# One attention-decode kernel: TensorE's two visits taken out of the loop around all engines, its closing branch followed by an aligned block, and five memsets moved from VectorE to GpSimd

## The chip, the cores and the metric

The kernel runs on one core of one Trainium2 chip. The metric is the device time of one execution in microseconds. The time before is the median of three runs. The profile is of one further execution of the same program: its span runs from the first to the last instruction that the profiler recorded in the kernel, and the execution's own time is longer than the span, because something lies ahead of the first instruction and behind the last one. The engines are named as in the profile: PE (TensorE; PEld is its weight loads), DVE (VectorE), ACT (ScalarE), POOL (GpSimd) and SP (SyncE, which issues nearly all DMAs here). A letter q behind a name (SPq, PEldq) marks work of the engine's sequencer: branches, register moves, semaphore waits, DMA issues.

## What is computed

One decode step for one token with 32 heads, a cache of 8192 positions and head size 128, all in float32, and beside it a gated unit:

```
xn = layernorm(x)                                   # x: 1 x 1 x 512
q  = (xn @ wq), 32 heads of 128
o  = softmax(q . k_cache * 128**-0.5) . v_cache     # 8192 positions per head
s  = o @ wo
g  = silu((sigmoid(xn @ w_gate) * (xn @ w_up)) @ w_down)
out = x + s * g
```

The two caches are 32 x 8192 x 128 float32 each, 134 MB apiece. With the weights the kernel reads 293.67 MB and writes 2 KB.

## The kernel before

**Tiling.** The heads are taken in 16 pairs. A pair's keys are one load of 8 MB into one of three slots of SBUF, 128 partitions by 16384 numbers; a pair's values are another such load. Keys alternate between slots 0 and 1, values go to slot 2; the last pair's keys and values come in halves.

**Stages of a pair.** DVE multiplies the keys in place by the pair's query (L380) and sums each row of 128 (L381), so that every partition holds 128 scores, and takes their maximum (L383). PE turns and spreads the maxima, ACT forms the powers with exp (L397), PE multiplies them with the values (32 matmuls onto `po`), ACT copies `po` (L402), PE picks the parts, and DVE scales and turns the pair's output (L387 to L390). `scores(i)` of one pair runs ahead of `heads_out(i - 1)` of the pair before.

**Start.** Before the first pair DVE clears some tiles (L217 to L232), cuts `pick` out of the identity (L234), turns `x` once its load has come (L241), and forms the layer norm; then it scales `wq` (L266, L267), and PE sums the columns into the queries. The gate's weights are treated the same way.

**End.** After the last pair PE multiplies the heads' outputs with `wo`, which comes in six loads (`W_ENDS`), DVE does the last product and sum (L471, L473), and SP stores the result (L489).

**Order of the loads.** SP issues everything in one order written by hand: `wq`, `w_gate`, `w_up`, the first keys; then each load behind a wait for the engine that frees its slot (`load_keys(i, summed[i - 2])`, `load_values(i - 1, (valued, i - 1))`).

**Control flow.** All engines run a block `body` that ends in a closing branch (L493) back to its own start; the register `once` is 0 at the start and 1 at the end, so the branch falls through and the body runs once. On ACT, DVE and PE a hint instruction further up names that branch ahead of time (`mark_branch_hint_location`). PE's instructions are written down with `Later`, an object that notes calls and plays them later. PE plays them inside the body so: a loop of two visits (L477) around a conditional block (L478). On visit 0 the block is skipped, so PE jumps to the loop's end and back; on visit 1 it runs `before` (everything up to the first pair) and then a loop of 15 rounds over `each` (one pair). Behind that loop stand PE's hint, `last` (the last pair) and `after` (the product with `wo`).

**Behind the closing branch** stands the block `done`: SP clears the semaphores (L501), all engines meet in a barrier (drains at L101), SP waits there for the result's store as well, and a second barrier of all engines (L528) ends the kernel.

The two visits in the code:

```
with nc.Fori(0, 2, engines=pe_only) as visit:
    with PE.engine.If(visit > 0):
        PE.play(before)
        with nc.Fori(0, NP - 1, engines=pe_only):
            PE.play(each)
hints[PE.engine] = PE.engine.mark_branch_hint_location()
PE.play(last)
PE.play(after)
```

Of the kernel before, what the change touches and what calls it, by code (L numbers as in the profile page):

```python
# [10 lines left out]
ALU = mybir.AluOpType  # L11
# [39 lines left out]
def kernel(  # L51
# [12 lines left out]
    nc = tc.nc  # L64
# [24 lines left out]

    W_ENDS, W_FOLD = (14, 24, 28, 30, 31, 32), 28  # L90

    DVE, ACT, SP, POOL = nc.vector, nc.scalar, nc.sync, nc.gpsimd
    PE = Later(nc.tensor)
    pe_only = OrderedEngineSet([nc.tensor.engine])

    s_out = tc.alloc_semaphore("s_out")
    ACT.nop().then_inc(s_out, 16)
    section = ctx.enter_context(ExitStack())  # L100
    section.enter_context(tc.tile_critical())  # L101

    def sb(name, *shape):
        return nc.alloc_sbuf_tensor(name, [P, *shape], F32)[:]
# [9 lines left out]
    pick, half = sb("pick", 2 * HT), sb("half", 2)  # L114
# [9 lines left out]
    weights = sb("weights", NB // HT, 2 * HT)  # L124
    sc = [sb(f"sc{i}", NB) for i in range(2)]
    on = sb("on", Dh)
# [28 lines left out]
    pe, dve, act, pool = (Steps(n) for n in ("s_pe", "s_dve", "s_act", "s_pool"))  # L155
# [10 lines left out]
    def wait(eng, *steps):  # L166
        for s in steps:
            if s is not None:
                eng.wait_ge(*s)
# [26 lines left out]
    def load_keys(i, *after):  # L196
        n = (i + 1) % 2
        wait(SP, *after)
        ld_k[i] = [(j, load(SP, f"k{n}_{j.start}", slots[n][:, cols(j)], rows_of(k_cache, i)[:, cols(j)]))
                   for j in (FULL if i < NP - 1 else HALVES)]  # L200

    def load_values(i, *after):
# [2 lines left out]
        SP.dma_start(slots[2], rows_of(v_cache, i)).then_inc(s_val, 16)  # L205

    load_keys(0)


    once = nc.alloc_registers("once")  # L210
    nc.regs_mov(once, 0)
    nc.br("body")
    body = ctx.enter_context(ExitStack())
    body.enter_context(nc.body("body"))
    hints = {e: e.mark_branch_hint_location() for e in (ACT, DVE)}

    c_xrow = dve(DVE.memset(x_row, 0.0))  # L217
    ld_xr = load(ACT, "xr", x_row[0:P:GP, :], xv.rearrange("(g c) -> g c", g=NG), c_xrow)
# [2 lines left out]
    c_id = pool(POOL.memset(ident, 0.0))  # L221
    wait(POOL, c_id)
    c_id = pool(POOL.affine_select(out=ident, in_=ident, compare_op=ALU.not_equal, fill=1.0, base=0,
                                   pattern=[[-1, P]], channel_multiplier=1))
    dve(DVE.memset(acc, 0.0))
    dve(DVE.memset(po, 0.0))
    dve(DVE.memset(weights, 0.0))
    dve(DVE.memset(on, 0.0))
    c_half = dve(DVE.memset(half, 0.0))
    wait(DVE, c_id, c_half)  # L230
    for e, h in enumerate(HALF):
        dve(DVE.memset(half[h, e:e + 1], 1.0))  # L232
    for g in range(NG):
        c_pick = dve(DVE.tensor_copy(pick[g * GP:(g + 1) * GP, :],  # L234
                                     ident[g * GP:(g + 1) * GP, g * GP:g * GP + 2 * HT]))
# [6 lines left out]
    t = dve(DVE.reduce_sum(st[:, 0:1], x_col, axis=AX.X))  # L242
    wait(PE, t)
    t = pe(PE.matmul(pt[:, 0:1], ones, st[:, 0:1], start=True, stop=True))
    wait(DVE, t)
# [6 lines left out]
    t = dve(DVE.reduce_sum(st[:, 2:3], sq, axis=AX.X))  # L252
    wait(PE, t)
    t = pe(PE.matmul(pm[:, 0:1], ones, st[:, 2:3], start=True, stop=True))
    wait(ACT, t, c_eps)
# [7 lines left out]
    def in_place(w, k, cols=slice(None)):  # L263
        y = w[:, 0, cols]
        if k == 0:
            return dve(DVE.tensor_scalar(y, y, xn[:, 0:1], None, op0=ALU.mult))  # L266
        return dve(DVE.scalar_tensor_tensor(y, w[:, k, cols], xn[:, k:k + 1], y, op0=ALU.mult, op1=ALU.add))  # L267
# [8 lines left out]
    for t in range(NQ):  # L276
        c = slice(t * QT, (t + 1) * QT)
        wait(PE, in_place(wq_t, KT - 1, c), copies.get(t - 2))
        spreads[t] = pe(PE.matmul(big[t % 2], ones, wq_t[:, 0, c], start=True, stop=True))
        wait(ACT, spreads[t])  # L280
# [74 lines left out]
                            start=(b == 0), stop=(b == HT - 1))  # L355
        ins.then_inc(picked, 1)

    wait(PE, c_pick, c_id)
    before = PE.take()
    pair(slots[2], {0: lambda: taken(s_val, 16)})  # L360
    each = PE.take()
# [112 lines left out]
    after = PE.take()  # L474


    with nc.Fori(0, 2, engines=pe_only) as visit:  # L477
        with PE.engine.If(visit > 0):  # L478
            PE.play(before)
            with nc.Fori(0, NP - 1, engines=pe_only):  # L480
                PE.play(each)
    hints[PE.engine] = PE.engine.mark_branch_hint_location()
    PE.play(last)
    PE.play(after)

    SP.wait_ge(s_out, 16)
    SP.nop().then_inc(s_out, -16)
    wait(SP, t)
    SP.dma_start(out.rearrange("a b (g c) -> (a b g) c", g=NG), g_row[0:P:GP, :]).then_inc(s_out, 16)  # L489

    nc.regs_alu(once, once, 1, op=ALU.add)
    for e in (ACT, DVE, PE.engine, POOL, SP):
        br = e.br_lt(once, 1, on_true="body", on_false="done")  # L493
        if e in hints:
            br.branch_hint(hints[e])
    body.close()
    nc.switch_bb("done")

    used = sorted(s.num for s in sems)
    assert used == list(range(used[0], used[0] + len(used)))  # L500
# [32 lines left out]
```

## Time and profile before

| | us |
|---|---|
| median of 3 runs | 689.98 (689.77 to 690.3) |
| the profiled execution, its own time | 690.04 |
| its span | 685.7 |
| own time less span | 4.3 |
| DVE busy | 606.2 (88% of the span) |
| PE busy | 211.8 (31%) |
| POOL busy | 0.7 (six instructions) |
| memory read | 293.67 MB, 428 GB/s over the span |

How to read it: an engine's busy time is that of its computing instructions alone. A wait is the idle time of an engine ahead of an instruction, with what ended it. The chain that ended last is followed back from the last instruction. For DMA queues the profile gives packets, megabytes and the time that the packets took as a share of 16 DMA engines over the stretch asked for. Queue q1 carries SP's loads, q10 the load of `x`, and q8 and q14 carry packets of the kind "instruction", that is, program text.

### The profile page before, as it was taken

How to read it: one execution, taken by the hardware profiler on the slowest of the kernel's cores; microseconds unless marked ns; L12 is line 12 of the kernel's file. 1: busy time of each engine (PE TensorE's matmuls, PEld its weight loads, DVE VectorE, ACT ScalarE, POOL GpSimd, SP SyncE). 2: the span in 40 equal slices, each digit the busy share in tenths (PEclk: the TensorE clock that was granted, in tenths of full speed). 3: DMA queues.
4: the chain of work that ended last, by engine and by line, in shares of the span. 5: the costliest groups of instructions: out<-in, count | busy, mean ns of one | idle time of the engine just before them, and what ended most of it. 6: DMA issues, size and time to landing. Idle time of an engine off the chain costs nothing.

```text
span 685.7 us, 3402 instructions
## 1 busy us (share of the span) xinstructions
PE 211.8 (31%) x1422; PEld 74.8 (11%) x1422; DVE 606.2 (88%) x166; ACT 39.9 (6%) x120; POOL 0.7 (0%) x6
## 2 busy tenths in 40 slices
PE   0242015060512306050512406050522406060476
PEld 0010001020101102020100101020100102010121
DVE  3876999999999899998989899898989899899931
ACT  0030010000010100000000100000010100000010
POOL 0000000000000000000000000000000000000000
PEclk9975557575665757575665757575575757575698
DMA  8999999999999999999999999999999999999996
GB/s 368 433 446 428 463 432 428 428 428 428 428 432 428 443 459 440 428 428 428 428 428 432 428 440 455 447 428 428 428 428 428 432 428 428 466 417 459 400 428 278
DMA packets 6610, 293.71 MB, mean 428 GB/s; under 512 B 744, under 2 KB 752, under 8 KB 1232
## 3 DMA queue, kind: packets, MB, share of 16 engines
q1 hardware_dynamic: 6600, 293.67, 99.1%
q8 instruction: 2, 0.03, 0.0%
q10 hardware_dynamic: 8, 0.00, 0.0%
HBM read 293.67 MB, written 0.00 MB: 428 GB/s over the span
## 4 chain that ended last, share of the span: by engine, by line
DVE 51%; DMA 35%; SPq 0%; issue 0%; PE 0%
DMA slot<-in_A_k_cache_dram 31%; DVE sc L381 25%; DVE slot L380 25%; DMA slot<-in_A_wo_dram 4%; SPq L163 0%; DVE on L388 0%; DVE o_t L390 0%; DVE mx L372 0%; DVE mx L383 0%; PE pt L37 0%; PE acc L37 0%; DVE g_row L471 0%; DVE g_row L473 0%; DVE rl L387 0%; DVE g_row L417 0%
## 5 line engine op out<-in xcount | busy, mean ns | idle before, releaser
L380 DVE TENSOR_TENSOR slot<-slot,q_all 128x16384 f32<-128x16384 f32 (+1 forms) x17 | 275.6, 16214 | 34.0 <-DMA slot<-in_A_k_cache_dram 34.0
L381 DVE TENSOR_REDUCE sc<-slot 128x128 f32<-128x16384 f32 (+1 forms) x17 | 275.7, 16216 | 0.6
L37 PE MATMUL po<-slot,weights 128*8 128x512 f32 x1024 | 146.8, 729 | 263.9 <-PEq L37 263.9
L37 PEld LDWEIGHTS po<-slot,weights 128*8 128x8 f32 x1024 | 45.5, 102 | 351.9 <-issue 345.1
L37 PE MATMUL pt<-ident,mx 128*1 128x128 f32 x32 | 8.6, 367 | 107.8 <-PEq L37 107.8
L402 ACT COPY o<-po 128x512 f32<-128x512 f32 x16 | 9.4, 587 | 416.9 <-PE po L37 416.9
L267 DVE SCALAR_TENSOR_TENSOR slot<-slot,xn 128x512 f32<-128x512 f32 (+2 forms) x16 | 24.3, 1554 | 3.0 <-DMA slot<-in_A_wq_dram 2.7
L37 PE MATMUL pn<-o,pick 128*2 128x128 f32 x128 | 16.5, 272 | 12.8 <-PEq L37 12.8
L37 PE MATMUL big<-slot,ones 128*128 128x512 f32 (+3 forms) x52 | 12.2, 496 | 25.5 <-DVE slot L267 23.6
L37 PEld LDWEIGHTS pt<-ident,mx 128*1 128x1 f32 x32 | 1.8, 80 | 112.0 <-issue 112.0
L37 PEld LDWEIGHTS pn<-o,pick 128*2 128x2 f32 x128 | 9.9, 84 | 29.5 <-issue 27.1
L387 DVE RECIPROCAL rl<-pn 2x1 f32<-2x1 f32 x16 | 2.3, 146 | 12.2 <-PE pn L37 12.2
L397 ACT ACTIVATE weights<-sc,nb 64x128 f32<-64x128 f32 x32 | 12.8, 401 | 0.9
L395 ACT ACTIVATE nb<-pm 128x2 f32<-128x2 f32 x16 | 2.8, 173 | 150.8 <-PE pm L37 150.8
L37 PE MATMUL pm<-mx,ones 1*128 1x2 f32 x32 | 8.6, 337 | 7.8 <-PEq L37 7.8
L471 DVE TENSOR_TENSOR g_row<-g_row,acc 128x128 f32<-128x128 f32 x1 | 0.3, 289 | 11.7 <-PE acc L37 11.7
L37 PE MATMUL pn<-rs,half 128*2 128x1 f32 x32 | 3.0, 163 | 23.7 <-PEq L37 23.7
L37 PE MATMUL big<-slot,o_all 128*1 128x512 f32 x56 | 8.9, 725 | 2.8 <-DMA slot<-in_A_wo_dram 2.8
L37 PE MATMUL big<-slot,o 128*1 128x512 f32 (+1 forms) x22 | 4.5, 934 | 16.3 <-DMA slot<-in_B_w_down_dram 16.3
L37 PEld LDWEIGHTS pm<-mx,ones 1*128 1x128 f32 x32 | 7.7, 298 | 14.6 <-issue 14.6
L37 PEld LDWEIGHTS big<-slot,ones 128*1 128x1 f32 (+1 forms) x52 | 4.0, 133 | 34.2 <-DVE slot L267 28.3
L283 ACT COPY q_all<-big 64x256 f32<-64x256 f32 x16 | 5.9, 368 | 23.1 <-PE big L37 22.6
(56 smaller groups left out, 52.5 us busy)
## 6 DMA issues: line engine op xcount, KB each, us to landing
slot<-in_A_wq_dram SPq DMA_DIRECT2D x2, 4096.0 KB, 18.2
slot<-in_A_k_cache_dram SPq DMA_DIRECT2D x2, 4096.0 KB, 37.8
slot<-in_A_v_cache_dram SPq DMA_DIRECT2D x2, 4096.0 KB, 37.8
slot<-in_A_wo_dram SPq DMA_DIRECT2D x1, 3584.0 KB, 15.4
slot<-in_B_w_gate_dram SPq DMA_DIRECT2D x1, 2752.0 KB, 28.9
slot<-in_B_w_up_dram SPq DMA_DIRECT2D x1, 2752.0 KB, 34.9
slot<-in_B_w_down_dram SPq DMA_DIRECT2D x1, 2560.0 KB, 22.0
slot<-in_A_wo_dram SPq DMA_DIRECT2D x1, 2560.0 KB, 21.1
```

The costliest lines, as they stand in the source:

```text
L37: ins = getattr(self.engine, name)(*args, **kwargs)
L267: return dve(DVE.scalar_tensor_tensor(y, w[:, k, cols], xn[:, k:k + 1], y, op0=ALU.mult, op1=ALU.add))
L283: copies[t] = act(ACT.copy(qb[h, 2 * t:2 * t + 2, :], q[h, :, e, :]))
L380: wait(DVE, dve(DVE.tensor_mul(k[:, j, :], k[:, j, :], qb[:, i:i + 1, :].to_broadcast([P, n, Dh]))))
L381: summed[i] = dve(DVE.reduce_sum(sc[i % 2][:, j], k[:, j, :], axis=AX.X))
L387: wait(DVE, dve(DVE.reciprocal(rl[:2], pn[:, Dh:])))
L395: wait(ACT, act(ACT.mul(nb, pm, -SCALE)))
L397: ACT.activation(weights[h, :, e * HT:(e + 1) * HT], sc[i % 2][h].rearrange("p (g b) -> p g b", b=HT), AF.Exp, bias=nb[h, e:e + 1], scale= ...
L402: ACT.copy(o1, po).then_inc(copied, 1)
L471: t = dve(DVE.tensor_mul(g_row, g_row, acc))
```

## The change

Four things are done.

1. All five engines' instructions in the body are noted with `Later` and played afterwards; only the first loads of SP (`first_loads`) are played ahead, where they stood. Each engine keeps its order.
2. PE's two visits come ahead of the body. A PE-only block `visit` skips its content while PE's register `pe_once` is 0, counts it up and jumps back while it is under 2. Only then do all engines go into `body`, which for PE now holds the hint, `last` and `after` alone. The other engines set `once` to 1 with a move ahead of the body, where they had set it to 0, and the addition at the end (L491) is gone on all engines.
3. Behind `done`, PE's next instruction is put at the start of a new block of 256 instructions (`addr_align(256)`); the gap is filled with no-ops.
4. The memsets of `weights`, `on` and `half` (one and two halves) go from DVE to POOL, behind POOL's work on the identity; PE's wait ahead of the first pair is for the last of them instead of the identity. DVE no longer waits for its own memset of `half`.

```diff
-    DVE, ACT, SP, POOL = nc.vector, nc.scalar, nc.sync, nc.gpsimd
-    PE = Later(nc.tensor)
+    DVE, ACT, SP, POOL, PE = (Later(e) for e in (nc.vector, nc.scalar, nc.sync, nc.gpsimd, nc.tensor))
...
-    ACT.nop().then_inc(s_out, 16)
+    nc.scalar.nop().then_inc(s_out, 16)
+    once = nc.alloc_registers("once")
+    pe_once = next(r for r in once if r.engine == nc.tensor.engine)
+    nc.reg_mov(pe_once, 0)
...
     load_keys(0)
-    once = nc.alloc_registers("once")
-    nc.regs_mov(once, 0)
-    nc.br("body")
-    body = ctx.enter_context(ExitStack())
-    body.enter_context(nc.body("body"))
-    hints = {e: e.mark_branch_hint_location() for e in (ACT, DVE)}
+    first_loads = SP.take()
...
-    dve(DVE.memset(weights, 0.0))
-    dve(DVE.memset(on, 0.0))
-    c_half = dve(DVE.memset(half, 0.0))
-    wait(DVE, c_id, c_half)
+    pool(POOL.memset(weights, 0.0))
+    pool(POOL.memset(on, 0.0))
+    wait(POOL, pool(POOL.memset(half, 0.0)))
     for e, h in enumerate(HALF):
-        dve(DVE.memset(half[h, e:e + 1], 1.0))
+        c_pool = pool(POOL.memset(half[h, e:e + 1], 1.0))
+    wait(DVE, c_id)
...
-    wait(PE, c_pick, c_id)
+    wait(PE, c_pick, c_pool)
...
-    with nc.Fori(0, 2, engines=pe_only) as visit:
-        with PE.engine.If(visit > 0):
+    SP.play(first_loads)
+    for r in once:
+        if r.engine != nc.tensor.engine:
+            nc.reg_mov(r, 1)
+    nc.br("visit", engines=pe_only)
+    with nc.body("visit", valid_engines=pe_only):
+        with PE.engine.If_ne(pe_once, 0):
             PE.play(before)
             with nc.Fori(0, NP - 1, engines=pe_only):
                 PE.play(each)
-    hints[PE.engine] = PE.engine.mark_branch_hint_location()
+        PE.engine.reg_alu(pe_once, pe_once, 1, ALU.add)
+        PE.engine.br_lt(pe_once, 2, on_true="visit", on_false="visited")
+    nc.switch_bb("visited")
+    nc.br("body")
+    body = ctx.enter_context(ExitStack())
+    body.enter_context(nc.body("body"))
+    hints = {e: e.mark_branch_hint_location() for e in (nc.scalar, nc.vector, nc.tensor)}
+    for e in (ACT, DVE, POOL, SP):
+        e.play(e.take())
     PE.play(last)
     PE.play(after)
+    SP = nc.sync
...
-    nc.regs_alu(once, once, 1, op=ALU.add)
...
     nc.switch_bb("done")
+    nc.tensor.addr_align(256)
```

More of the change, by code (lines that the diff above doesn't have):

```diff
@@ L489 @@
     SP.dma_start(out.rearrange("a b (g c) -> (a b g) c", g=NG), g_row[0:P:GP, :]).then_inc(s_out, 16)
-    nc.regs_alu(once, once, 1, op=ALU.add)
-    for e in (ACT, DVE, PE.engine, POOL, SP):
+    for e in (nc.scalar, nc.vector, nc.tensor, nc.gpsimd, nc.sync):
         br = e.br_lt(once, 1, on_true="body", on_false="done")
```

## The prediction

> **What bounds the kernel now.** I read the span first, then the windows by stage, then both ends, since the change touches only the two ends.
>
> ```profile
> span 685.7 us, 3402 instructions
> ```
>
> ```profile
> core 0: us, PE busy (x) PEld busy (x) DVE busy (x) ACT busy (x) POOL busy (x), PEclk, DMA share, GB/s
> 0.00:8.00 8.00, 0.00 (x0) 0.00 (x0) 2.15 (x14) 1.28 (x1) 0.70 (x6) 1.00 0.85 326
> 8.00:92.00 84.00, 18.26 (x80) 5.83 (x80) 66.53 (x34) 8.76 (x21) 0.00 (x0) 0.73 1.00 431
> 92.00:234.00 142.00, 44.84 (x311) 16.63 (x310) 141.34 (x25) 8.28 (x25) 0.00 (x0) 0.64 1.01 436
> 234.00:620.00 386.00, 116.57 (x781) 42.77 (x782) 357.57 (x74) 17.47 (x60) 0.00 (x0) 0.63 1.00 433
> 620.00:656.00 36.00, 11.61 (x80) 4.46 (x79) 35.83 (x10) 1.75 (x6) 0.00 (x0) 0.62 1.01 437
> 656.00:686.00 30.00, 20.56 (x174) 5.10 (x172) 2.81 (x12) 2.33 (x7) 0.00 (x0) 0.87 0.78 334
> ```
>
> The last two columns decide. From 8 to 656 us the DMA engines are full (share 1.00 or 1.01) at 431 to 437 GB/s. DVE is busy for nearly all of 92 to 234 us too, but the queue loses nothing by that. So the loads set the 648 us between, and no edit changes a load, its order or what it waits for. What is left to win or lose is how early the first load is issued, and what follows the last one.
>
> The end, from the chain of waits in order of time and from the lines of the closing branch (L493), the two barriers (L101, L528) and the store:
>
> ```profile
> 657.68 24.18 DMA slot<-in_A_wo_dram
> ...
> 681.91 0.44 PE acc L37 x8
> ...
> 682.70 0.29 DVE g_row L473
> ```
>
> ```profile
> 683.02 0.65 SPq L489 DMA_DIRECT2D out_dram<-g_row  x1
> ```
>
> ```profile
> L493 PEldq COMPARE_BRANCH  x1: 83/83/83, 682.0 to 682.0; - x1
> ```
>
> ```profile
> L101 SPq EVENT_SEMAPHORE  x4: 17/22/360, 684.0 to 684.3; - x4
> ...
> L101 PEldq DRAIN  x1: 8/8/8, 684.0 to 684.0; - x1
> ```
>
> ```profile
> L528 PEldq DRAIN  x2: 8/66/124, 684.3 to 685.2; - x2
> ...
> L528 PEldq EVENT_SEMAPHORE  x2: 51/51/51, 685.0 to 685.6; - x2
> ```
>
> PE passes its closing branch at 682.0 us (83 ns) and then stands for 1.9 us, until its drain runs at 684.0. SP is the late one: it stores at 683.02, and its last wait at L101, the 360 ns one that starts at 684.3, ends at about 684.7. I read that wait as the landing of the store, since the drains of the others were over by then. So PE has slack behind its branch: 1.9 us before its drain is asked for, about 2.6 us before SP looks for it last. The span ends at 685.7.
>
> Now the program text that is fetched, first in the window 0 to 8 us, then in 684 to 688, then in 685 to 685.1 (40 slices of 2.5 ns):
>
> ```profile
> q8 instruction: 1, 0.02, 0.7%
> ```
>
> ```profile
> q8 instruction: 1, 0.02, 1.9%
> q14 instruction: 1, 0.01, 0.8%
> ```
>
> ```profile
> DMA  0000000000000000000900000000000000000000
> ```
>
> Queue q8 carries two packets of 0.02 MB (16 KB), and I take them for PE's, since its text is much the longest. The second starts in the twentieth slice, at 685.05 us. Its share of 1.9% of 16 engines over 4 us is 0.019 x 16 x 4 = 1.2 us, so it lands at about 686.3, which is 0.6 us behind the last instruction of the span. That is the one thing of PE's that reaches past the end, and the execution's own time runs on for 690.04 - 685.7 = 4.3 us around the span. It starts 1.0 us behind PE's drain at 684.0 and 2.9 us behind its closing branch. The drain at 684.3 is the odd one out as well: 124 ns against 8 ns for the other, so I take 684.0 to 684.3 as the place where PE's sequencer asked for the block.
>
> **The change part by part.** The memsets first. DVE and POOL at the start:
>
> ```profile
> 1.45 0.29 POOL L223 TENSOR_SCALAR_AFFINE_SELECT ident<-ident 128x128 f32<-128x128 f32 x1 [0.22 <-POOL ident L221]
> ...
> 2.31 0.27 DVE L227 MEMSET weights<- 128x256 f32 x1
> ...
> 3.08 0.74 DVE L234 COPY pick<-ident 32x8 f32<-32x8 f32 x4
> 8.24 0.40 DVE L241 STREAM_TRANSPOSE g_row<-x_row 128x128 f32<-128x128 f32 x1 [4.42 <-DMA x_row<-in_A_x_dram]
> ```
>
> DVE loses 3.08 - 2.31 = 0.77 us of work, so `pick` is done at about 3.05 instead of 3.82. Then it waits for `x` until 8.24 anyway: 4.42 us of idle time become 5.2, and the gain is 0. If that cover were gone, the price would still be 0, because DVE next waits for `wq`:
>
> ```profile
> 14.67 2.35 DVE L266 TENSOR_SCALAR slot<-slot,xn 128x4096 f32<-128x4096 f32 x1 [2.94 <-DMA slot<-in_A_wq_dram]
> ```
>
> On POOL the five come behind 1.45 + 0.29 = 1.74 us. A POOL memset of 128x128 has its row in the groups by line:
>
> ```profile
> L221 POOL MEMSET ident<- 128x128 f32 x1 | 0.2, 205 | 0.6 <-SPq L101 0.6
> ```
>
> So `weights` is at most twice 205 ns, `on` 205, the three small ones about 100 each, by the constants that POOL clears at the start:
>
> ```profile
> L519 POOL MEMSET const-float32-0.0<- x1: 99/99/99, 0.2 to 0.2; 128x1 f32 x1
> ```
>
> That is 0.9 us, done by 3 us. The first reader is PE's pair, tens of microseconds later. Even ten times the price is hidden. Nothing stands behind POOL's new wait but its own last two memsets, and PE's exchanged wait stands ahead of the first pair, when POOL is long done. Nothing is issued from POOL. Cost 0.
>
> The loads. SP's five first loads are played where they stood, ahead of its one register move, and nothing else is moved past SP's queue. PE gets a move ahead of the section; the move that it replaces stood behind:
>
> ```profile
> L477 PEldq MOVE  x3: 29/35/35, 1.1 to 2.2; - x3
> ```
>
> ```profile
> L478 PEldq COMPARE_BRANCH  x2: 77/218/358, 1.3 to 2.3; - x2
> ```
>
> ```profile
> 0.95 0.86 SPq L163 DMA_DIRECT2D slot<-in_A_wq_dram  x2
> ```
>
> A move is 29 to 35 ns. SP opens the section without waiting for PE, so its first load stays at 0.95 us and the cost is 0. If PE were waited for, the 35 ns would be paid in full, because the queue is full from then on.
>
> The two visits. Visit 0 still jumps over the same block and back at the same place of PE's stream, and PE's first matmul still waits for DVE, which turns `x` until 8.24 + 0.40 = 8.64. The branch of the condition takes 358 ns and 77 ns, the last at 2.3 us, so 6 us hide it in either form. Two moves less on PE are hidden too. The additions gone at L491 are worth about 45 ns on SP, ahead of its wait for the store: hidden by that wait, 0.
>
> **The block behind the closing branch** is what is left. PE's matmuls are 165 calls, each two weight loads and two matmuls (32 calls a pair make 1024 matmuls in 16 pairs, so 64 a pair), 660 instructions, and some 40 others: about 700, of which some 690 stand ahead of the aligned place. With blocks of 256 that place is instruction 768, less what the runtime has put in front, so the gap is at most 78 no-ops. No row shows PE's no-op. The nearest are SP's 13 to 18 ns and PE's semaphore wait of 51 ns:
>
> ```profile
> L101 SPq NOP  x2: 13/16/18, 0.7 to 684.7; - x2
> ```
>
> The ends are 0 (no gap) and 78 x 51 ns = 4.0 us; I take half the gap at PE's move of 30 ns, 39 x 30 = 1.2 us, under the 1.9 us of slack. Then the fetch. Before, PE asked for its next block when its drain was released, at 684.0. In the new kernel PE crosses into the next block right behind the branch, at 682.0 to 683.2. With the same 1.0 us until the packet starts and the same 1.2 us of packet it lands at 684.2 to 685.4, against about 684.7 when SP's wait for the store ends: between 0 and 0.7 us late, 0.2 in the middle. And the 0.6 us by which the block landed past the span are no longer there to be waited for. Sum against the profiled execution: 690.04 + 0.2 - 0.6 = 689.6. That execution is 0.06 us above the median of the runs, so the forecast for the median is **689.6**, its own range 689.1 to 690.4. A difference of 0.2% (1.4 us) is about what a measurement of this kernel can tell from no change.
>
> **The rivals.**
>
> *PE waits for its block, and the end waits for PE (slower).* The fetch may have been asked for at the closing branch and not at the drain: then it took 685.05 - 682.0 = 3.0 us to start and 4.3 to land. PE needs the block at once in the new kernel, since its drain of L101 stands in it, and SP's barrier needs that drain. It would be there at 686.3 instead of 684.7: +1.6 us, less up to 0.6 at the tail, so 691.0 to 691.6. It decides from the point where the block lands later than 684.7. For it: no row shows when PE asked. Against it: the long drain at 684.3, and 3.0 us is long for an idle queue (the store took 0.65 us to issue and had landed 1.0 us later).
> [...]
>
> *The no-ops are on the path.* 78 of them at 51 ns are 4.0 us, past the slack by 2.1, and the fetch may only start behind them: 690.04 + 2.1 + 2.2 - 0.6 = 693.7 at worst; with 60 at 35 ns it is about 691.5.
>
> *Nothing changes.* What lies behind the span may wait for another engine (q14's packet of 0.8%, 0.5 us, comes in that window too), so the earlier fetch is hidden: 690.0. I count this with the forecast's range.
>
> *A larger gain.* If the tail of 4.3 us waited for PE with more than the 0.6 us, or DVE's shorter text (five memsets and an addition fewer) spares it a fetch like q14's, one to two microseconds go: 688.3 to 689.
>
> **How the numbers follow.** Forecast with "nothing changes" 0.68; PE waits for its block 0.16; no-ops 0.06; larger gain 0.10. The range takes the forecast's, reaches up into the first rival and down into the larger gain: 688.7 to 691.2. Faster by over 0.2% (under 688.6) is the lower half of the larger gain and a little drift, 0.07; slower (over 691.4) is part of the first rival and most of the no-ops, 0.13; within 0.2% the rest, 0.80.
>
> **What would show it.** Right: the middle stages' DMA share and the start of `scores` unchanged; q8's second packet at 683 to 684.5 us instead of 685.05; PE's drain of L101 still near 684 and SP's last wait no later than about 685; own time less span smaller than 4.3. Wrong: PE's drain at 686 (first rival), no-ops on PE over more than 2 us (second), q8's packet where it was, or a first load later than 0.95 us. The memsets are right if DVE's wait ahead of L241 grows to about 5.2 us and L266 still starts at about 14.7.

## The result, and the profile after

The kernel after takes 689.18 us (median of 20 runs, 688.25 to 689.87); the kernel before, measured 20 times beside it, 690.42 us (689.62 to 691.24). The ratio is 0.9981, its 95% interval 0.9974 to 0.9988: 1.24 us faster, just under the 0.2% that the prediction set as its bound. In the profiled executions the sum is 690.04 to 688.92, but its two terms go opposite ways and are both larger than it:

| | before | after |
|---|---|---|
| profiled execution | 690.04 | 688.92 |
| span | 685.7 | 687.1 |
| time less span | 4.3 | 1.8 |

So the kernel proper became 1.4 us longer, and what lies around it 2.5 us shorter. I call the time less the span the **tail** from here on, although it also holds whatever lies ahead of the first instruction. Over the runs it is 4.2 to 5.8 us before (median 4.9, 63 runs timed beside the experiments) and 1.8 in all 20 runs after. The span scatters after the change: 686.5 to 688.1 us with a median of 687.4, against 685.2 to 685.9 with a median of 685.6 before. By the medians the two terms are thus +1.8 and -3.1 us.

The start and the middle of the kernel after, from the windows by stage and the timeline (all noted instructions now carry the helper's line, L37, so they are told by their tiles):

```profile
8.00:92.00 84.00, 18.23 (x80) 5.76 (x80) 66.54 (x34) 8.73 (x21) 0.00 (x0) 0.73 1.00 432
92.00:234.00 142.00, 45.85 (x311) 15.61 (x310) 141.48 (x25) 8.24 (x25) 0.00 (x0) 0.64 1.00 435
234.00:620.00 386.00, 115.39 (x781) 43.37 (x782) 357.63 (x74) 17.38 (x60) 0.00 (x0) 0.63 1.00 433
```

```profile
0.97 0.86 SPq L37 DMA_DIRECT2D slot<-in_A_wq_dram  x2
...
1.69 0.31 POOL L37 MEMSET weights<- 128x256 f32 x1
...
1.94 0.20 POOL L37 MEMSET on<- 128x128 f32 x1
2.08 0.42 POOL L37 MEMSET half<- 128x2 f32 x3
```

```profile
2.17 0.75 DVE L37 COPY pick<-ident 32x8 f32<-32x8 f32 x4
8.13 0.40 DVE L37 STREAM_TRANSPOSE g_row<-x_row 128x128 f32<-128x128 f32 x1 [5.21 <-DMA x_row<-in_A_x_dram]
...
14.55 2.35 DVE L37 TENSOR_SCALAR slot<-slot,xn 128x4096 f32<-128x4096 f32 x1 [2.93 <-DMA slot<-in_A_wq_dram]
```

The memory queue is as full as it was (share 1.00 at 432 to 435 GB/s). The memsets are done on POOL by 2.5 us, DVE's wait for `x` grew from 4.42 to 5.21 us, and `wq` is waited for as long as before (2.93 for 2.94 us). The last sum of the chain starts where it did, too:

```profile
681.91 0.44 PE acc L37 x8
...
682.70 0.29 DVE g_row L37
```

All of the difference lies behind that. TensorE's closing branch (now L500), its no-ops (L505), the first barrier (now L102) and SP's waits:

```profile
L500 PEldq COMPARE_BRANCH  x1: 73/73/73, 681.9 to 681.9; - x1
```

```profile
L505 PEldq NOP  x13: 13/13/13, 682.1 to 683.1; - x13
```

```profile
L102 SPq EVENT_SEMAPHORE  x4: 17/22/28, 683.9 to 686.1; - x4
...
L102 PEldq DRAIN  x1: 8/8/8, 686.0 to 686.0; - x1
```

```profile
SPq L497 <- DVE g_row L37: 24.8, 1, 24.8
SPq L102 <- PEq L102: 1.9, 1, 1.9
```

Before, SP's last wait at this barrier was the store's:

```profile
SPq L101 <- DMA out_dram<-g_row: 0.4, 1, 0.4
```

Now it waits 1.9 us for PE, whose drain runs at 686.0 instead of 684.0. The program text, in the window 683 to 684.7 us (40 slices of 42.5 ns):

```profile
DMA  0000000000000009000000000000001000000000
...
q8 instruction: 1, 0.02, 3.5%
```

PE's block starts in the sixteenth slice, at 683.65 us, 0.5 us behind the last no-op, and takes 0.035 x 16 x 1.7 = 1.0 us, to 684.6. PE runs on at 686.0, so 1.4 us pass between the packet's end and PE's next instruction. The kernel before had a packet of q14 behind its span; the window 687.7 to 687.8 us shows its start:

```profile
DMA  0009000000000000000000000000000000000000
...
q14 instruction: 1, 0.01, 33.2%
```

In the kernel after, a window from 684.7 to 692 us has no packet at all:

```profile
DMA packets 0, 0.00 MB, mean 0 GB/s; under 512 B 0, under 2 KB 0, under 8 KB 0
```

### The profile page after: what moved, and what is told of

The parts are those of the page before. It is cut to its first block, busy times and chain, and to the rows that moved or that the text cites. A ratio compares the mean times of both kernels' runs of the same rounds, so it can differ in the third digit from the quotient of the medians.

```text
span 687.1 us, 3406 instructions
## 1 busy us (share of the span) xinstructions
PE 211.5 (31%) x1422; PEld 74.5 (11%) x1422; DVE 605.9 (88%) x161; ACT 39.7 (6%) x120; POOL 1.4 (0%) x11
## 4 chain that ended last, share of the span: by engine, by line
DVE 51%; DMA 34%; SPq 0%; issue 0%; PE 0%
DMA slot<-in_A_k_cache_dram 31%; DVE sc L37 25%; DVE slot L37 25%; DMA slot<-in_A_wo_dram 4%; DVE mx L37 0%; SPq L37 0%; DVE on L37 0%; DVE o_t L37 0%; DVE g_row L37 0%; PE pt L37 0%; PE acc L37 0%; DVE rl L37 0%
## 5 line engine op out<-in xcount | busy, mean ns | idle before, releaser
L37 DVE TENSOR_TENSOR slot<-slot,q_all 128x16384 f32<-128x16384 f32 (+1 forms) x17 | 275.6, 16214 | 34.0 <-DMA slot<-in_A_k_cache_dram 34.0
L37 DVE TENSOR_REDUCE sc<-slot 128x128 f32<-128x16384 f32 (+1 forms) x17 | 275.7, 16216 | 0.6
L37 PE MATMUL po<-slot,weights 128*8 128x512 f32 x1024 | 147.9, 734 | 264.1 <-PEq L37 264.1
L37 PEld LDWEIGHTS po<-slot,weights 128*8 128x8 f32 x1024 | 45.5, 103 | 353.2 <-issue 347.1
L37 PE MATMUL pt<-ident,mx 128*1 128x128 f32 x32 | 9.1, 385 | 108.2 <-PEq L37 108.2
L37 ACT COPY o<-po 128x512 f32<-128x512 f32 x16 | 9.4, 585 | 418.2 <-PE po L37 418.2
L37 DVE SCALAR_TENSOR_TENSOR slot<-slot,xn 128x512 f32<-128x512 f32 (+2 forms) x16 | 24.3, 1554 | 3.0 <-DMA slot<-in_A_wq_dram 2.6
L37 PE MATMUL pn<-o,pick 128*2 128x128 f32 x128 | 16.5, 272 | 12.7 <-PEq L37 12.7
L37 PE MATMUL big<-slot,ones 128*128 128x512 f32 (+3 forms) x52 | 12.1, 493 | 25.6 <-DVE slot L37 23.7
L37 DVE RECIPROCAL rl<-pn 2x1 f32<-2x1 f32 x16 | 2.3, 146 | 13.7 <-PE pn L37 13.7
L37 PEld LDWEIGHTS pt<-ident,mx 128*1 128x1 f32 x32 | 1.8, 80 | 112.5 <-issue 112.5
L37 PEld LDWEIGHTS pn<-o,pick 128*2 128x2 f32 x128 | 9.9, 84 | 29.5 <-issue 27.1
L37 ACT ACTIVATE weights<-sc,nb 64x128 f32<-64x128 f32 x32 | 12.8, 399 | 0.9
L37 ACT ACTIVATE nb<-pm 128x2 f32<-128x2 f32 x16 | 2.8, 172 | 151.4 <-PE pm L37 151.4
L37 PE MATMUL pm<-mx,ones 1*128 1x2 f32 x32 | 8.6, 337 | 7.6 <-PEq L37 7.6
L37 PE MATMUL pn<-rs,half 128*2 128x1 f32 x32 | 3.0, 163 | 23.5 <-PEq L37 23.5
L37 PE MATMUL big<-slot,o 128*1 128x512 f32 (+1 forms) x22 | 4.4, 923 | 16.3 <-DMA slot<-in_B_w_down_dram 16.3
L37 PEld LDWEIGHTS pm<-mx,ones 1*128 1x128 f32 x32 | 7.7, 298 | 14.9 <-issue 14.9
L37 DVE TENSOR_TENSOR g_row<-g_row,acc 128x128 f32<-128x128 f32 x1 | 0.3, 287 | 10.1 <-PE acc L37 10.1
L37 ACT COPY q_all<-big 64x256 f32<-64x256 f32 (+1 forms) x17 | 6.4, 379 | 34.4 <-PE big L37 33.9
L37 PE MATMUL big<-slot,o_all 128*1 128x512 f32 x56 | 7.2, 591 | 3.0 <-DVE o_all L37 1.9
L37 PEld LDWEIGHTS big<-slot,ones 128*1 128x1 f32 (+1 forms) x52 | 4.0, 131 | 34.2 <-DVE slot L37 28.9
```

The lines of the kernel that those rows point to most:

```text
L37: ins = getattr(self.engine, name)(*args, **kwargs)
```

## The experiments

Two things had changed at once in the tail: TensorE's packet had come forward, and q14's had gone. A block here is the piece of program text that one such packet brings: in the trace of before a slice of 2.5 ns shows 6554 GB/s for q8's (685 to 685.1 us) and 3277 for q14's (687.7 to 687.8), which makes 16 KB and 8 KB. Theory P: the tail waited for TensorE's block, which the aligned block brings forward. Theory V: it waited for VectorE's text. VectorE's program is seven instructions shorter (five memsets, a wait and an addition), and could have run over into a block that the instructions behind the kernel had to wait for. All kernels here were timed beside the kernel before, whose median was 690.28 to 690.46.

**The memsets alone** (before, plus this):

```diff
-    dve(DVE.memset(weights, 0.0))
...
+    pool(POOL.memset(weights, 0.0))
...
-    wait(PE, c_pick, c_id)
+    wait(PE, c_pick, c_pool)
```

> The kernel before, with only the five memsets moved from VectorE to GpSimd (VectorE's text six instructions shorter). What is looked at is the time less the span (4.3 us before, 1.8 us after) and the packet of instruction queue q14 at 687.7 us, which is there before and gone after. Theory V (VectorE's text: the 4.3 us held a fetch for an engine whose text ran over into another block behind the kernel, and the shorter text spares it): span 685.7, time less span between 1.8 and 2.5, time 687.5 to 688.2, q14's late packet gone. Theory P (TensorE's text: the 4.3 us waited for TensorE's block, which the new kernel asks for earlier): as before, 685.7 + 4.3 = 690.0, q14's packet still there.

Measured 690.15 us, ratio 0.9994 (0.9985 to 1.0003), span 685.6, tail 3.2 to 5.2 with a median of 4.7. The window 684 to 692 us, in slices of 0.2 us:

```profile
DMA  0000000000000000030000000000000000000000
...
q8 instruction: 1, 0.02, 0.8%
```

q14's packet is gone, as V has it, and the time is P's: TensorE's block starts at about 687.4 and the tail is as long as ever.

**TensorE's part alone** (after, with the memsets back on VectorE):

```diff
+    dve(DVE.memset(weights, 0.0))
...
-    wait(PE, c_pick, c_pool)
+    wait(PE, c_pick, c_id)
```

> The kernel after, with the five memsets back on VectorE: TensorE's part of the change alone. Theory V: span 687.1 as after, time less span 4.3 as before, 691.4 in all, q14's late packet back. Theory P: span 687.1, time less span 1.8, 688.9 as after.

Measured 691.27 us, ratio 1.0011 (1.0002 to 1.002), span 686.9 in the profiled execution, tail 4.0 to 4.4. In 684 to 692 us:

```profile
DMA  0000000000000000000000001000000000000000
...
q14 instruction: 1, 0.01, 0.4%
```

This is V's outcome: TensorE's block came inside the span, and the tail is long all the same.

**VectorE's text padded** (after, plus seven memsets of unread numbers):

```diff
     c_eps = dve(DVE.memset(eps_t, EPS))
+    for n in range(9, 16):
+        dve(DVE.memset(st[:, n:n + 1], 0.0))
```

> The kernel after, with seven more memsets of one column each, of numbers that nothing reads, on VectorE behind the constant for the layer norm, so that VectorE's text is as long as before while the five memsets stay on GpSimd. They take some 0.4 us under the 5 us in which VectorE waits for x. Theory V: the length alone decides, span 687.1, time less span 4.3, 691.4. Theory P: 688.9 as after.

Measured 691.16 us, ratio 1.0013 (1.0004 to 1.0022), tail 4.2 to 4.4. The five memsets are on GpSimd here, and the seven others cost nothing where they stand. The packet is back, at about 689.1 (slice 26):

```profile
DMA  0000000000000000000000000100000000000000
...
q14 instruction: 1, 0.01, 0.4%
```

So the length of VectorE's text decides, not the work that left it. Neither theory holds alone, since the memsets alone gave nothing. What fits all three runs is theory B: the end waits for whichever of two late blocks comes last, TensorE's or VectorE's, and only a kernel that is rid of both has the short tail.

**Without TensorE's hint** (after, minus one hint and hinted branch):

```diff
-    hints = {e: e.mark_branch_hint_location() for e in (nc.scalar, nc.vector, nc.tensor)}
+    hints = {e: e.mark_branch_hint_location() for e in (nc.scalar, nc.vector)}
```

> The kernel after without the hint instruction for TensorE's closing branch; the aligned block stays. If the hint is what kept TensorE's next block from being fetched in sequence, q8's second packet comes when TensorE enters its third block (around 655 to 665 us) and not at 683.7, TensorE's drain in the first barrier runs at 684.0 instead of 686.0, and SP's wait is for the store again: span 685.6 to 685.8, time less span 1.8 by both theories, 687.5. If the hint has nothing to do with it: as after, 687.1 and 688.9.

Measured 687.47 us, ratio 0.9954 (0.994 to 0.9968), span 685.5, tail 1.8 to 2.0. In 666 to 667 us:

```profile
q8 instruction: 1, 0.02, 6.0%
```

```profile
L102 SPq EVENT_SEMAPHORE  x4: 17/22/360, 683.8 to 684.2; - x4
...
L102 PEldq DRAIN  x1: 8/8/8, 683.8 to 683.8; - x1
```

The block now starts at about 666.7 us, 16 us before the last no-op at 682.9. The aligned block and its no-ops (14 here) are still there, and PE's drain runs at 683.8, with those of the other engines: the no-ops cost nothing where the block has come early. SP's longest wait at the barrier is the store's again (0.4 us). This is faster than both kernels.

**Without the aligned block** (after, with the hint):

```diff
-    nc.tensor.addr_align(256)
```

> The kernel after without the aligned block: TensorE's closing branch falls through as before and the next block is reached only behind the kernel. Theory B (either text is enough: the end waits for whichever engine's next block comes last, TensorE's or VectorE's): span 685.6 as before, TensorE's late fetch behind the kernel again (q8's second packet at 685 to 687.5), time less span 4.2 to 5, time 689.8 to 690.6, as with the memsets moved alone. Theory V alone (the block of TensorE costs nothing behind the kernel): 685.6 + 1.8 = 687.4.

Measured 689.87 us, ratio 0.9988 (0.9977 to 0.9999), span 685.7, tail scattered from 1.9 to 5.4. The window 684 to 692 us:

```profile
DMA  0000000000300000000000000000000000000000
...
q8 instruction: 1, 0.02, 0.9%
```

The median fits theory B, though the tail scatters further down than the 4.2 to 5 that was expected: with VectorE's text short, the tail is TensorE's alone. The packet starts at 686.0 to 686.2 in this execution, whose tail was 2.8; in the run with the memsets alone it started at 687.4, and the tail was 4.6. What is short in a few runs here is short in all runs with the alignment: it turns a scattered 1.9 to 5.4 into a steady 1.8, and pays for it in the span, whose median is 687.4 instead of 685.5.

**The aligned block alone** (before, plus it):

```diff
     nc.switch_bb("done")
+    nc.tensor.addr_align(256)
```

> The kernel before with the aligned block behind its closing branch, nothing else. Theory B: the stall of TensorE comes into the span (687.1) and VectorE's stays behind it (4.0 to 4.4): 691.2 to 691.5, as in the run with TensorE's part alone, so that taking the two visits out of the body is worth nothing. If the visits' place matters: another time by more than 0.5.

Measured 691.62 us, ratio 1.0016 (1.0007 to 1.0025), span 687.1, tail 4.2 to 4.5, with q14's packet behind the span (window 688 to 692 us):

```profile
q14 instruction: 1, 0.01, 0.7%
```

As expected, but for 0.1 us more. With the visits ahead of the body it was 691.27, and the two kernels' runs overlap (691.28 to 692.2 and 690.66 to 691.95). Against the kernel before that was timed beside each they lose 1.16 and 0.99 us: taking the visits out of the body shows no gain beyond the noise.

**Before, without VectorE's and TensorE's hints:**

```diff
-    hints = {e: e.mark_branch_hint_location() for e in (ACT, DVE)}
+    hints = {e: e.mark_branch_hint_location() for e in (ACT,)}
...
-    hints[PE.engine] = PE.engine.mark_branch_hint_location()
```

> The kernel before without the hint instructions and hinted branches on VectorE and TensorE (ScalarE keeps its own); memsets, visits and block as before. Theory H (the hint keeps the engine from fetching the next block in sequence, so that it is fetched only when the engine gets there): both blocks come early, span 685.6, time less span 1.8, 687.4; q8's second packet around 655 to 670 us, no packet of q14 behind the span. If the hints don't matter on VectorE: 689.7 to 690.

Measured 687.57 us, ratio 0.9956 (0.9942 to 0.9969), span 685.8, tail 1.8 to 2.0. The first row is from the window 60 to 61 us, the second from 665 to 667:

```profile
q14 instruction: 1, 0.01, 1.9%
```

```profile
q8 instruction: 1, 0.02, 3.0%
```

With neither memsets moved nor a block aligned nor a visit displaced, both packets come early: VectorE's at 60 to 61 us, while it multiplies the first keys, TensorE's at about 666.0, when the last pair runs. Nothing of either queue is left behind 684 us. That the late q14 packet is VectorE's, which the padded run showed by the length, is shown here a second time together with the run without TensorE's hint alone, below: it moves with VectorE's hint.

**The plain form** (after, without hint, alignment and first visit of TensorE):

```diff
-        with PE.engine.If_ne(pe_once, 0):
-            PE.play(before)
-            with nc.Fori(0, NP - 1, engines=pe_only):
-                PE.play(each)
-        PE.engine.reg_alu(pe_once, pe_once, 1, ALU.add)
+        PE.play(before)
+        with nc.Fori(0, NP - 1, engines=pe_only):
+            PE.play(each)
+        PE.engine.reg_alu(pe_once, pe_once, 2, ALU.add)
...
-    nc.tensor.addr_align(256)
```

> The kernel after without TensorE's hint, without the aligned block and without the first of the two visits (TensorE runs the content once): memsets on GpSimd stay. Theory H: 685.5 + 1.8 = 687.4, as with the hint alone taken out: neither visit nor alignment is worth anything then. q8's first packet comes only when TensorE first enters its second block, at some 60 to 95 us in the first pair. If the early visit is needed to keep TensorE from a stall in the first pair that reaches the loads: over 687.9.

Measured 687.39 us, ratio 0.9953 (0.994 to 0.9967), span 685.8, tail 1.8. In 104 to 106 us, and then in 666 to 668:

```profile
q8 instruction: 1, 0.02, 3.2%
```

```profile
q8 instruction: 1, 0.02, 3.0%
```

The first packet comes at about 105 us instead of 4.2 (the kernel after) or 6.7 (before), a little later than I had put it, and costs nothing. This is the lowest median of the study, but its lead over the two other kernels in which both packets are early or gone and the span is as before (687.47 and 687.57) is no larger than their runs scatter.

**Before, without TensorE's hint alone:**

```diff
-    hints[PE.engine] = PE.engine.mark_branch_hint_location()
```

> The kernel before without TensorE's hint alone; VectorE's hint, the memsets and the visits as before. Theory B with H: TensorE's second packet comes at 655 to 670 us, VectorE's packet of q14 stays behind the span, 685.6 + 4.1 = 689.7, and the times scatter less than before's, as in the run with TensorE's part alone (4.0 to 4.4). If TensorE's block alone made the 4.3: 687.4.

Measured 689.99 us, ratio 0.9996 (0.9987 to 1.0005), span 685.6, tail 4.2 to 4.8. In 684 to 692 us:

```profile
DMA  0000000000000000001003000000000000000000
...
q8 instruction: 1, 0.02, 0.8%
q14 instruction: 1, 0.01, 0.4%
```

VectorE's packet at 687.7 is still there, and the tail stays long, as expected, though it reaches up to 4.8 and not 4.4. Another packet of q8, at 688.2, I had not expected. The kernel without both hints has the same TensorE text, a tail of 1.8 and no such packet, so the end does not need it there; whether the few longer tails here wait for it is not shown.

**Before, a second trace:**

> The kernel before once more, for a second trace of it. In the first trace q8's second packet came at 685.05 us, 2 us earlier than in the run with only the memsets moved, whose TensorE text is the same. If that start scatters from execution to execution, it comes elsewhere between 685 and 687.5 here; if it belongs to the kernel, at 685.0 to 685.1.

One execution, 690.57 us, tail 5.0. In 684 to 692 us:

```profile
DMA  0000000000000000031000000000000100000000
...
q8 instruction: 1, 0.02, 0.9%
q14 instruction: 2, 0.02, 0.8%
```

TensorE's packet starts at 687.4 here, against 685.05 in the trace that the prediction read: its start scatters by over 2 us from execution to execution of one program, and it did not belong to PE's drain at 684.0. VectorE's does not scatter so: in all six traces that have it behind the span, it starts about 2 us behind the span's end. What the second packet of q14 is, at 690.3 us, stays open.

The runs in one table; a block is "in time" when its packet came before the end of the loads, and "spared" when no packet of q14 came for it at all:

| kernel | TensorE's block | VectorE's block | span (median) | tail (median) | time |
|---|---|---|---|---|---|
| before | behind the kernel | behind | 685.6 | 4.9 | 690.42 |
| memsets alone | behind | spared | 685.6 | 4.7 | 690.15 |
| before without TensorE's hint | in time | behind | 685.6 | 4.4 | 689.99 |
| before without both hints | in time | in time | 685.7 | 1.8 | 687.57 |
| aligned block alone | in the span | behind | 687.3 | 4.3 | 691.62 |
| TensorE's part alone | in the span | behind | 687.1 | 4.1 | 691.27 |
| after, padded VectorE | in the span | behind | 686.9 | 4.4 | 691.16 |
| after | in the span | spared | 687.4 | 1.8 | 689.18 |
| after without alignment | behind | spared | 685.5 | 4.5 | 689.87 |
| after without TensorE's hint | in time | spared | 685.5 | 1.8 | 687.47 |
| plain form | in time | spared | 685.6 | 1.8 | 687.39 |

The spans quoted with the runs above are of the profiled execution alone, these are medians over all runs. The tails bear theory B out in one more way: with VectorE's block alone late and TensorE's in the span they lie between 4.0 and 4.5 us, with TensorE's alone between 1.9 and 5.4, and the kernel before, which has both, never falls under 4.2: the scatter of the one on the floor of the other.

## Why the prediction was right, and where it was wrong

**Right:** the forecast of a small gain, 689.6 for a measured 689.18 and a range of 688.7 to 691.2. The bound by the loads, the memsets' work at no gain and no cost, the start of the first load (0.95 forecast, 0.97 measured, with a move more on PE), and the place: all of the difference comes from the text that is fetched behind the closing branch. The reading of SP's last wait as the landing of the store was right as well. The no-ops (13, spread over 1.0 us) fit the forecast's 1.2 us, but that they are hidden is shown only where TensorE's hint is out; in the kernel after they stand between the branch and the packet, and whether they delay it is not shown.

**Wrong, and it matters more than the hit:** the two terms of the sum. "+0.2" for the block's lateness was +1.4 in the span, and "-0.6" at the tail was -2.5. The two errors, +1.2 and -1.9, leave -0.7 between them, and only so did the forecast stay near: that was luck. By the prediction's own sign, PE's drain at 686, the first rival had come true, and the larger gain made up for it.

- The first was the step "with the same 1.0 us until the packet starts and the same 1.2 us of packet it lands at 684.2 to 685.4". The packet came as early as that (683.65 to 684.6). What failed is that landing was taken for the moment at which PE can run: 1.4 us more passed. The three other kernels with the aligned block and the hint lost as much in the span (medians 686.9 to 687.3, for 685.6 before). The first rival had the right mechanism (PE waits for its block, and the end for PE, drain at 686.0, span +1.4) by a wrong reason: it put the request too early, not the restart too late. Its 691.0 to 691.6 is what TensorE's part alone measured, 691.27.
- The second was the step from the packet's end at 686.3 to "0.6 us", which put the tail down to PE alone; q14's packet was seen and set aside under "nothing changes" and "a larger gain". In the execution that the prediction read, the 4.3 us were most likely VectorE's and not PE's: its q14 packet stands where it stands in the kernels with VectorE's block alone late, whose tails are 4.0 to 4.5, while TensorE's packet came early, about 1 us earlier against the span's end than in the run without alignment, whose tail was 2.8. This is argued from the packets' places, since the instructions behind the kernel are not listed. So the rival "a larger gain" had the truth in its second half: VectorE's shorter text spares a fetch.
- "I take 684.0 to 684.3 as the place where PE's sequencer asked for the block": fallen. The second trace of the same program has the packet 2.4 us later, so a start in one trace was chance and not a place.
- The sum treated the memsets' 0 and the block's gain as separate. They are not: the memsets alone give 0.1 us within the interval, TensorE's part alone loses 1.0, and both together gain 1.24, because the tail is the later of two waits.
- One sum among the rivals is off: 60 no-ops at 35 ns come by its own terms to 690.04 + 0.2 + 2.2 - 0.6 = 691.8, not 691.5. Nothing else rests on it.

So falling through into the next block cost TensorE nothing where its hint was out: in the kernel after without the hint the packet starts 16 us ahead of the last no-op, and the drain runs at 683.8. In the kernel after, with the hint, the same fall-through took 2.9 us from the last no-op (683.1) to the drain (686.0). The 256 instructions to a block, with which the forecast counted, agree with these two traces: in the kernel after, 124 matmuls, 116 weight loads and 13 no-ops of PE are listed from 666.7 us on, where the packet starts without the hint, up to the aligned place, 253 in all. The gap was 13 no-ops, not up to 78; what stands ahead of PE's own text, which the forecast left open, no trace lists.

What stays open: why 1.4 us pass between the packet's end and PE's next instruction; how the hint keeps the next block away, since the runs show only that it comes late with the hint (683.65 us) and early without (666.7); why the start of TensorE's packet scatters behind the kernel; and how far the instructions behind the kernel, which the trace does not list, run into the new blocks. VectorE's margin is bracketed only: one instruction less than before (TensorE's part alone) is not enough, six (the memsets alone) are.

## What to carry to other kernels

Look at the time less the span before anything else at the end of a kernel: 2.5 to 3 us sat there that no engine's row showed, and the DMA view's packets of the kind "instruction" gave it away. A hinted closing branch that was not taken cost this kernel a fetch just where nothing was left to hide it; try it without the hint before you move instructions about to suit a block's boundary (687.5 against 689.2). And where an end waits for the later of two things, an edit that removes one of them can measure as nothing, so test them together.

## What the runs showed of the hardware that was not expected

- With a hint on the closing branch, which falls through, the packet of the next block came late, and without it early, on TensorE (683.7 us in the kernel after, 666.0 to 667.0 in three kernels without the hint) and on VectorE (687.7 in the kernel before, 60 to 61 without the hint).
- In the kernel after, whose block starts to come only at 683.65 us, TensorE's next instruction (686.0) runs 2.9 us behind its last no-op (683.1); the packet itself is 1.0 us of that.
- The late packet of VectorE started about 2 us behind the span's end in six traces (687.71 for a span of 685.7 in the first), while TensorE's started anywhere from 0.6 us ahead of it to 1.8 us behind it in four.
- TensorE's no-ops are listed with 13 ns each, but 13 of them spread from 682.1 to 683.1 us: some 80 ns apart.
- Seven instructions more or less on VectorE, at the very start of the kernel, decided 2 us at its very end (691.16 against 689.18).
